# First layer's 147 contraction rows in one full pass and a quarter-array group, with slots of four chunks

## The chip, the cores and the metric

The kernel runs on one core of one Trainium2 chip. The metric is the device time of one execution in microseconds. Five engines work beside each other, each through its own queue in order: TensorE (PE, with its weight loads shown apart as PEld), VectorE (DVE), ScalarE (ACT), GpSimd (POOL) and SyncE (SP), which here only issues DMA transfers.

## The reference

Attention through 49 agents, then two dense layers over 12480 tokens of 128 values.

```python
def sm(a, b):
    s = scale * (a @ b.transpose(0, 2, 1))
    s = s - s.max(-1, keepdims=True)
    e = np.exp(s)
    return e / (e.sum(-1, keepdims=True) + 1e-09)
a2k = sm(agents, k)
agent_v = a2k @ v
q2a = sm(q, agents)
x = q2a @ agent_v                                   # 12480 x 128
h = x @ moe_w_in                                    # 128 -> 2048
g = np.where(h > 0, h, np.exp(np.minimum(h, 0)) - 1)
x = g @ moe_w_out                                   # 2048 -> 128
h = x @ moe2_w_in                                   # 128 -> 2048
g = np.maximum(h, 0) + moe2_alpha * np.minimum(h, 0)
out = g @ moe2_w_out                                # 2048 -> 128
```

## The kernel before

**Precision.** Matrix products run in fp32r, a float32 form with fewer mantissa bits, and get back what is lost by splitting: a value is written as a high part (its fp32r rounding) and a low part (the rest). A product of two split operands is three matmuls, high x high, high x low, low x high (`mm3`).

**First layer, folded.** The kernel multiplies `agent_v` with the first layer's weights once (the end of `prologue`), so that the first layer for a token is a product of its 49 softmax weights with a 49 x 2048 matrix. `pst[b]` holds the softmax weights of a block, transposed: 64 partitions with the high parts (49 agents, padded to 64), 64 with the low parts. `s1` holds the folded weights' high parts, the 49 rows once for each half, and `s1l` the low parts in the same layout. `g1` multiplies both with `pst`: two matmuls of 128 contraction rows for each chunk of 128 hidden values, 16 chunks (`NF`) a block.

**Blocks, units, slots.** The tokens come in 25 blocks (`BLOCKS`: ten of 480, fifteen of 512). Two chunks make a unit; a block has eight units (`NP`), the kernel 200 (`U`). `slot(s)` issues the work of one step: `g1` of unit s and its activations; `g1_elu` of unit s-1, which gives `g`, its fp32r rounding `gh` (on DVE for even units, on ACT for odd ones) and the rest `gl` (POOL); `g2` of unit s-`D1` (second matrix of the first layer, 6 matmuls, accumulated over the block in one PSUM bank `y`); `g3` of unit t = s-`L2` (first matrix of the second layer, 6 matmuls, and `xh` on ACT, `xl` on DVE); `g4` of unit t-`D2` (last matrix, 6 matmuls, accumulated in bank `o`, with three more for the linear part at the block's end, a copy and the store). `e` is made by two ACT steps, Relu and Exp.

**PSUM.** Eight banks: `y`, `o`, and a ring of three pairs (`hpair`), which `g1`, `g3` and `q_scores` take in turn. A pair comes free when the last engine that reads it is done.

**Softmax of later blocks.** `queries(t)` spreads the softmax of a coming block over the slots, by the table `Q_STEPS`, in units of one chunk: scores (two matmuls, L157 and L158, step 3), maximum, exponential, sum, normalisation, transposition, and at last `q_hi` (ACT) and `q_lo` (POOL), which write `pst`.

**Order.** In the prologue and the first `AUTO` slots a planner orders every engine's queue but SP's, which is as written; after these, all queues are in the order of the code. In the first slots `micro` also issues parts of `decode`, which turns the 64-bit words of the remaining weight slices into float32 high and low parts, on DVE, ACT, POOL and PE. `PE_LO` names the slices whose low part PE makes.

Of the kernel before, what the change touches and what calls it, by code (L numbers as in the profile page):

```python
# [15 lines left out]
P = 128  # L16
# [6 lines left out]
BLOCKS = [480] * 10 + [512] * 15  # L23
PIECES = [(i * 1280, 10, 128) for i in range(9)] + [(11520, 8, 120)]
NP = NF // 2
D1 = 2
D2 = 1
L2 = 11
Q_AHEAD = 24
NY = 2  # L30
WORK = 2
KRING = 4
# [7 lines left out]
    w9 w10 w11 w12 w13 w14 w15  # L40
"""
ORDER = """
    S0 T9 S1 Q2 T9 S2 Q2 T9 S3 Q2 S4 Q2 S5 Q2 D0 T9 S6 Q2 X0 E0 E1 T9 S7 Q2 T9 S8 Q2 E2 E3 T9 S9 T9 E4 A0 D1
# [15 lines left out]
def agent_attention_moe_kernel(  # L59
# [11 lines left out]
    alpha: bass.AP,  # L71
    outT: bass.AP,
):

# [16 lines left out]
    def bank(tag, bufs):  # L91
        if tag in ("m", "z"):
            return rings["mz"].tile([P, 512], F32, tag=tag, bufs=bufs, name=tag)
        return ps.tile([P, 512], F32, tag=tag, bufs=bufs, name=tag)

    def hpair():
        return rings["h"].tile([P, 2, 512], F32, tag="h", name="h")
# [5 lines left out]
        t0 += n  # L103
    NB = len(blocks)

    q_t, q_st, pst, y_ps, y_t, o_ps = {}, {}, {}, {}, {}, {}
    h_t, g_t, e_t, x_t, k_t = {}, {}, {}, {}, {}
    rings = {}

# [10 lines left out]
    s1l = const.tile([P, NF, P], F32R, name="s1l")  # L120
# [134 lines left out]
    def q_lo(b):  # L255
# [59 lines left out]
    def decode(i):  # L315
# [29 lines left out]
        parts = i in PE_LO  # L345
        u = a
        if parts:
            u = u1[j] if name == "wi1" else dec.tile([P, 4, P], F32R, tag="du", name="du")
# [70 lines left out]
    def micro(n):  # L419

        while n > 0:
            ran = False
            for x in list(flying):
                if next(x, "end") == "end":
                    flying.remove(x)
                ran = True
                n -= 1
            if len(flying) < 2 and started[0] in words:
                flying.append(decode(started[0]))
                started[0] += 1  # L430
            elif not ran:
                return
# [6 lines left out]
    w1, u1 = {}, {}  # L439

    def prologue():
        nc.sync.dma_start(out=agp, in_=agT)
        make_identity(nc, ident)
        nc.gpsimd.tensor_copy(out=plus, in_=ident)
        nc.vector.tensor_scalar(out=minus, in0=ident, scalar1=-1.0, scalar2=None, op0=ALU.mult)
        stages = [f for k in sorted(Q_STEPS) for f in Q_STEPS[k]]
        with tc.tile_pool(name="att", bufs=1) as att:
            with tc.tile_pool(name="kring", bufs=KRING) as kr, tc.tile_pool(name="vring", bufs=1) as vr, \
                    tc.tile_pool(name="sps", bufs=2, space=bass.MemoryType.PSUM) as sps, \
                    tc.tile_pool(name="mz", bufs=1, space=bass.MemoryType.PSUM) as mz:  # L450
# [9 lines left out]
                mx = att.tile([P, 2, A], F32, name="mx")  # L460
                for j in range(4):
                    w1[j] = att.tile([P, 4, P], F32, name=f"w1_{j}")
                    u1[j] = att.tile([P, 4, P], F32R, name=f"u1_{j}") if j in PE_LO else None
                pump()

                for t in range(2):
# [70 lines left out]
                for x in ORDER.split():  # L537
# [17 lines left out]
                    out=avs[:, 1, :], in0=av[1][:A, 0:P + 1], scalar=cs[:, 1:2], in1=avs[:, 0, :],  # L555
                    op0=ALU.mult, op1=ALU.add,
                )
                at = bank("o", 1)
                nc.tensor.transpose(at[:, 0:A], avs[:, 1, 0:P], ident[:A, :A])
                avn = att.tile([P, 2, AP], F32, name="avn")  # L560
                nc.gpsimd.memset(avn, 0.0)
                nc.vector.tensor_copy(out=avn[:, 0, :A], in_=at[:, 0:A])
                nc.scalar.copy(out=avn[:, 1, :A], in_=at[:, 0:A])
                avr = att.tile([P, 2, AP], F32R, name="avr")
                nc.vector.tensor_copy(out=avr, in_=avn)
                rs = att.tile([P, 1], F32, name="rs")
                nc.gpsimd.memset(rs, 0.0)
                nc.vector.tensor_scalar(out=rs[:A], in0=avs[:, 1, P:P + 1], scalar1=1e-9, scalar2=None, op0=ALU.add)
                nc.vector.reciprocal(out=rs[:A], in_=rs[:A])
                nc.vector.tensor_copy(out=rs[AP:], in_=rs[:AP])  # L570
            rings["h"] = ctx.enter_context(tc.tile_pool(name="hps", bufs=3, space=bass.MemoryType.PSUM))
            for j in range(4):
                if j % 2 == 0:
                    hp = hpair()
                wp = hp[:, j % 2, :]
                sl = slice(4 * j, 4 * j + 4)
                last = j not in PE_LO
                nc.tensor.matmul(
                    wp, avn.rearrange("p j a -> p (j a)"), w1[j].rearrange("p f c -> p (f c)"), start=True, stop=last
                )  # L580
                if not last:
                    nc.tensor.matmul(
                        wp, avr.rearrange("p j a -> p (j a)"), u1[j].rearrange("p f c -> p (f c)"),
                        start=False, stop=True,
                    )
                w4 = wp.rearrange("p (f c) -> p f c", c=P)
# [27 lines left out]
    def g1_elu(u):  # L614
        n = of(u)[2]
        g = wide("g", F32, n)
        e, h = e_t.pop(u), h_t.pop(u)
        nc.vector.scalar_tensor_tensor(out=g, in0=e, scalar=-1.0, in1=h, op0=ALU.add, op1=ALU.max)  # L618
        gh = wide("gh", F32R, n, D1 + 1)
        if u % 2:  # L620
            nc.scalar.copy(out=gh, in_=g)  # L621
        else:
            nc.vector.scalar_tensor_tensor(out=gh, in0=e, scalar=-1.0, in1=h, op0=ALU.add, op1=ALU.max)  # L623
        gl = wide("gl", F32R, n, D1 + 1)
        nc.gpsimd.tensor_tensor(out=gl, in0=g, in1=gh.bitcast(F32), op=ALU.subtract)  # L625
        g_t[u] = gh, gl

# [19 lines left out]
    def g3(u):  # L647
        b, i, n = of(u)
        yh, yl = y_t[b]
        h = hpair()[:, :, :n]  # L650
        assert WI2[i // 4] in done
        for c in range(2):
            mm3(h[:, c, :], wi2h[:, i + c, :], wi2l[:, i + c, :], yh[:, :n], yl[:, :n], True, True)
        xh, xl = wide("xh", F32R, n, D2 + 1), wide("xl", F32R, n, D2 + 1)
# [28 lines left out]
    def queries(t):  # L683
        b = t // NF
        if t % NF == 0:
            load_q(b + 2)
        for c in range(max(1, b), min(b + 3, NB)):
            for k in range(-NF, Q_AHEAD - NF) if t == 0 and c == 1 else ():
                for f in Q_STEPS.get(k, ()):
                    f(c)  # L690
            for f in Q_STEPS.get(t - NF * c + Q_AHEAD, ()):
                f(c)

    def slot(s):
# [12 lines left out]
        micro(MICRO)  # L707
        run(g1, s)
        run(g1_act, s)
        if s < U:  # L710
            queries(2 * s + 1)
        run(g4, t - D2)
        run(g2, s - D1)

    with tc.manual_schedule(engines=PINNED):
        for s in range(AUTO):
            slot(s)
    with tc.manual_schedule():
        for s in range(AUTO, U + L2 + D2):
            slot(s)  # L720


# [39 lines left out]
```

## Time and profile before

| what | value |
|---|---|
| median of 3 runs | 1191.17 us (1190.48 to 1193.3) |
| profiled execution | 1191.09 us |
| its span, first to last instruction | 1189.3 us |
| busy in the span | PE 94%, PEld 77%, DVE 68%, ACT 68%, POOL 54% |
| mean granted PE clock | 0.977 of full speed |

The profile is of one execution. A line of it names the line of the code, the engine, the operation, the tile written and those read, and the shape. Matmuls are pipelined: the distance between two starts tells the rate, and a matmul's own duration, with its modelled end, is longer. "Idle before" is the time in which the engine had nothing to do ahead of an instruction, and the name behind the arrow is what ended it.

### The profile page before, as it was taken

Reading aid. Unit: us, or ns where it says so; the run is one execution under the profiler, and the core shown is the slowest. Engines: PE = TensorE matmul, PEld = TensorE weight load, DVE = VectorE, ACT = ScalarE, POOL = GpSimd, SP = SyncE. Lnnn points to the kernel's source line nnn. Section 1 sums busy time; section 2 is a strip of 40 time slices with the busy share of each in tenths; the row PEclk is TensorE's granted clock in tenths of the full one; section 3 lists DMA queues with packets and bytes.
Section 4 is the critical chain, followed back from the end, with each engine's and each line's share of the span. In section 5 each row is a group of like instructions: output and inputs, shape, how many; then the busy total and the mean of one; then the engine's idle time right before and its main releaser. Section 6 shows DMA issues by size and latency. Waiting matters only on the chain.

```text
span 1189.3 us, 13141 instructions
## 1 busy us (share of the span) xinstructions
PE 1116.0 (94%) x4986; PEld 916.0 (77%) x4986; DVE 809.8 (68%) x977; ACT 806.2 (68%) x923; POOL 642.2 (54%) x351
## 2 busy tenths in 40 slices
PE   7866699999999999999999999999999999999998
PEld 6744588888888888878778778778777877878886
DVE  6979756666766676676667666666676667666653
ACT  3436577767776777777676777777677677777753
POOL 2667845455555555555554555555455555555530
PEclk9877799999999999999999999999999999999999
DMA  9860000000000000000000000000000000000000
GB/s 340 235 174 9 0 1 18 17 1 18 17 1 17 18 18 1 18 18 1 18 18 17 2 18 18 1 18 18 1 18 18 1 18 18 0 10 10 9 1 18
DMA packets 24077, 34.82 MB, mean 29 GB/s; under 512 B 1679, under 2 KB 16719, under 8 KB 24015
## 3 DMA queue, kind: packets, MB, share of 16 engines
q1 hardware_dynamic: 24015, 33.99, 9.0%
q8 instruction: 39, 0.64, 0.2%
q14 instruction: 23, 0.19, 0.0%
HBM read 27.60 MB, written 6.39 MB: 29 GB/s over the span
## 4 chain that ended last, share of the span: by engine, by line
PE 64%; DVE 21%; ACT 10%; issue 4%; DMA 1%; POOL 0%; SPq 0%; DVEq 0%; POOLq 0%; ACTq 0%
DVE g L618 6%; PE o L436 6%; PE o L437 6%; PE o L435 6%; PE h L435 6%; PE h L436 6%; PE y L435 6%; PE y L437 6%; PE y L436 6%; PE h L437 5%; PE h L605 5%; PE h L606 5%; DVE gh L623 5%; ACT e L612 2%; ACT gh L621 2%
## 5 line engine op out<-in xcount | busy, mean ns | idle before, releaser
L625 POOL TENSOR_TENSOR gl<-g,gh 128x1024 fp32r<-128x1024 f32 (+1 forms) x200 | 471.2, 2356 | 412.3 <-ACT gh L621 225.6
L656 DVE SCALAR_TENSOR_TENSOR xl<-h,xh 128x1024 fp32r<-128x1024 f32 (+1 forms) x200 | 239.0, 1195 | 238.4 <-ACT xh L655 236.7
L655 ACT ACTIVATE xh<-h 128x1024 fp32r<-128x1024 f32 (+1 forms) x200 | 200.2, 1002 | 126.7 <-PE h L437 126.6
L618 DVE SCALAR_TENSOR_TENSOR g<-e,h 128x1024 f32<-128x1024 f32 (+1 forms) x200 | 237.4, 1187 | 54.4 <-issue 26.0
L612 ACT ACTIVATE e<-e 128x1024 f32<-128x1024 f32 (+1 forms) x200 | 208.0, 1040 | 6.2
L611 ACT ACTIVATE e<-h 128x1024 f32<-128x1024 f32 (+1 forms) x200 | 200.0, 1001 | 10.4 <-PE h L606 5.1
L621 ACT CAST gh<-g 128x1024 fp32r<-128x1024 f32 (+1 forms) x100 | 102.8, 1028 | 150.7 <-DVE g L618 150.7
L605 PE MATMUL h<-pst,s 128*128 128x512 f32 (+1 forms) x400 | 158.2, 396 | 11.4 <-DVE gh L623 3.9
L435 PE MATMUL y<-gh,wo1h 128*128 128x512 f32 (+1 forms) x400 | 156.8, 392 | 5.6 <-DVE gh L623 5.6
L435 PE MATMUL h<-yh,wi2h 128*128 128x512 f32 (+1 forms) x400 | 156.1, 390 | 3.0 <-DVE g L618 3.0
L606 PE MATMUL h<-pst,s1l 128*128 128x512 f32 (+1 forms) x400 | 158.4, 396 | 0.0
L436 PE MATMUL y<-gl,wo1h 128*128 128x512 f32 (+1 forms) x400 | 157.3, 393 | 0.3 <-POOL gl L625 0.3
L437 PE MATMUL y<-gh,wo1l 128*128 128x512 f32 (+1 forms) x400 | 156.4, 391 | 0.0
L436 PE MATMUL o<-xl,wo2h 128*128 128x512 f32 (+1 forms) x400 | 155.7, 389 | 0.7 <-DVE xl L656 0.7
L437 PE MATMUL o<-xh,wo2l 128*128 128x512 f32 (+1 forms) x400 | 155.7, 389 | 0.0
L437 PE MATMUL h<-yh,wi2l 128*128 128x512 f32 (+1 forms) x400 | 155.6, 389 | 0.0
L435 PE MATMUL o<-xh,wo2h 128*128 128x512 f32 (+1 forms) x400 | 155.6, 389 | 0.0
L436 PE MATMUL h<-yl,wi2h 128*128 128x512 f32 (+1 forms) x400 | 155.6, 389 | 0.0
L623 DVE SCALAR_TENSOR_TENSOR gh<-e,h 128x1024 fp32r<-128x1024 f32 (+1 forms) x100 | 118.6, 1186 | 0.0
L605 PEld LDWEIGHTS h<-pst,s 128*128 128x128 f32 x400 | 76.4, 191 | 30.4 <-DVE gh L623 4.7
L435 PEld LDWEIGHTS y<-gh,wo1h 128*128 128x128 f32 x400 | 75.9, 190 | 21.8 <-issue 6.1
L435 PEld LDWEIGHTS h<-yh,wi2h 128*128 128x128 f32 x400 | 75.4, 188 | 19.3 <-ACT yh L643 3.4
(150 smaller groups left out, 1374.2 us busy)
## 6 DMA issues: line engine op xcount, KB each, us to landing
vt<-in_vm_dram SPq DMA_DIRECT2D x9, 640.0 KB, 7.1
kt<-in_kT_dram SPq DMA_DIRECT2D x8, 640.0 KB, 6.5
wi<-in_w_in_dram SPq DMA_DIRECT2D x8, 512.0 KB, 7.1
wo<-in_w_out_dram SPq DMA_DIRECT2D x8, 512.0 KB, 7.8
q<-in_qT_dram SPq DMA_DIRECT2D x15, 256.0 KB, 2.9
out_dram<-o SPq DMA_DIRECT2D x15, 256.0 KB, 2.0
q<-in_qT_dram SPq DMA_DIRECT2D x10, 240.0 KB, 3.2
out_dram<-o SPq DMA_DIRECT2D x10, 240.0 KB, 2.0
```

Source lines behind the costliest of these rows:

```text
L435: nc.tensor.matmul(out, w_hi, x_hi, start=start, stop=False)
L436: nc.tensor.matmul(out, w_hi, x_lo, start=False, stop=False)
L437: nc.tensor.matmul(out, w_lo, x_hi, start=False, stop=stop)
L605: nc.tensor.matmul(h_t[u][:, c, :], s1[:, i + c, :], pst[b][:, :n], start=True, stop=False)
L606: nc.tensor.matmul(h_t[u][:, c, :], s1l[:, i + c, :], pst[b][:, :n], start=False, stop=True)
L611: nc.scalar.activation(out=e, in_=h_t[u], func=AF.Relu, scale=-1.0)
L612: nc.scalar.activation(out=e, in_=e, func=AF.Exp, scale=-1.0)
L618: nc.vector.scalar_tensor_tensor(out=g, in0=e, scalar=-1.0, in1=h, op0=ALU.add, op1=ALU.max)
L623: nc.vector.scalar_tensor_tensor(out=gh, in0=e, scalar=-1.0, in1=h, op0=ALU.add, op1=ALU.max)
L625: nc.gpsimd.tensor_tensor(out=gl, in0=g, in1=gh.bitcast(F32), op=ALU.subtract)
L655: nc.scalar.activation(out=xh, in_=h, func=AF.Relu)
L656: nc.vector.scalar_tensor_tensor(out=xl, in0=h, scalar=0.0, in1=xh.bitcast(F32), op0=ALU.max, op1=ALU.subtract)
```

## The change

The first layer's contraction has 3 x 49 = 147 rows: high x high, high x low and low x high. The kernel before spends 256 rows on them, in two passes. The changed kernel puts 115 of them into one pass of 128 rows, and the other 32 into a 32-row matmul:

- `pst` keeps its 64 + 64 rows. The 15 padding agents are now copies of agents 0 to 14, so that rows 49 to 63 hold their high softmax weights again, which meet the low parts of the folded weights. Two more rows (agents 15 and 16) come by a small DMA. `Q0` = 17.
- `psq[b]` holds the high softmax weights of agents 17 to 48 four times, in partitions 0, 32, 64 and 96, by four DMAs (`q_place`, a new step behind `q_lo`).
- `s1q` holds the low parts for these 32 agents, of four chunks in the four groups of 32 partitions. `g1` now serves two units: four full matmuls and four of 32 contraction rows, each with its own partitions and PSUM bank.
- The end of the prologue normalises `agent_v` first, makes the quarter weights by 16 small matmuls into the four column groups (`hq`), and `s1` and `s1q` on DVE.
- A slot is two units (four chunks) long. `g1_split` is cut off from `g1_elu`. The order in a slot, the places of the softmax steps (`ask`), `L2` (11 to 10) and the rings of `gh`, `gl`, `xh`, `xl` change; `q_scores` falls at the end of a slot, behind `g4`.

```diff
-D1 = 2
-D2 = 1
-L2 = 11
+L2 = 10
+Q0 = 17
+GBUFS = 4
+XBUFS = 3
...
-PE_LO = (0, 2, 4)
+PE_LO = (4,)
...
-AUTO = 13
+AUTO = 12
...
+    def q_place(b):
+        n = blocks[b][1]
+        psq[b] = sm.tile([P, BLK], F32R, tag="psq", bufs=2, name="psq")
+        eng = nc.sync if b else nc.scalar
+        for g in range(4):
+            eng.dma_start(out=psq[b][32 * g:32 * g + 32, :n].bitcast(F32), in_=pst[b][Q0:A, :n].bitcast(F32))
+        eng.dma_start(out=pst[b][P - 15:P - 30 + Q0, :n].bitcast(F32), in_=pst[b][15:Q0, :n].bitcast(F32))
...
-        21: [q_lo],
+        21: [q_lo, q_place],
...
+        nc.scalar.copy(out=agp[:, A:], in_=agp[:, :AP - A])
...
+            hq = hpair()[:, 0, :].rearrange("p (k c) -> p k c", c=P)
+            hp = []
             for j in range(4):
                 if j % 2 == 0:
-                    hp = hpair()
...
-                nc.scalar.activation(out=s1[:, sl, :], in_=w4, func=AF.Copy, scale=rs)
+                for g in range(4):
+                    nc.tensor.matmul(
+                        hq[32 * g:32 * g + 32, j, :], avq[:, g, :], w1[j][:, g, :], start=True, stop=True
+                    )
+            hi = [att2.tile([P, 4, P], F32R, name=f"hi{j}") for j in range(2)]
+            nc.vector.tensor_copy(out=hi[1], in_=hq)
+            nc.vector.tensor_tensor(out=s1q, in0=hq, in1=hi[1].bitcast(F32), op=ALU.subtract)
+            for j in range(4):
+                w4 = hp[j // 2][:, j % 2, :].rearrange("p (f c) -> p f c", c=P)
+                nc.vector.tensor_copy(out=hi[j % 2], in_=w4)
                 nc.vector.scalar_tensor_tensor(
-                    out=s1l[:, sl, :], in0=w4, scalar=rs, in1=s1[:, sl, :].bitcast(F32),
-                    op0=ALU.mult, op1=ALU.subtract,
+                    out=s1[:, 4 * j:4 * j + 4, :], in0=hi[j % 2].bitcast(F32), scalar=low, in1=w4,
+                    op0=ALU.mult, op1=ALU.add,
                 )
...
     def g1(u):
         b, i, n = of(u)
-        h_t[u] = hpair()[:, :, :n]
-        for c in range(2):
-            nc.tensor.matmul(h_t[u][:, c, :], s1[:, i + c, :], pst[b][:, :n], start=True, stop=False)
-            nc.tensor.matmul(h_t[u][:, c, :], s1l[:, i + c, :], pst[b][:, :n], start=False, stop=True)
+        for v in range(2):
+            h_t[u + v] = hpair()[:, :, :n]
+            for c in range(2):
+                nc.tensor.matmul(h_t[u + v][:, c, :], s1[:, i + 2 * v + c, :], pst[b][:, :n], start=True, stop=False)
+        for g in range(4):
+            p = slice(32 * g, 32 * g + 32)
+            nc.tensor.matmul(
+                h_t[u + g // 2][:, g % 2, :], s1q[p, i // 4, :], psq[b][p, :n], start=False, stop=True
+            )
...
+        def ask(k):
+            micro(MICRO)
+            if s < U:
+                queries(2 * s + k)
+
         t = s - L2
-        micro(MICRO)
-        run(g1_elu, s - 1)
+        ask(0)
+        run(g1_split, s - 1)
         run(g3, t)
-        if s < U:
-            queries(2 * s)
-        micro(MICRO)
-        run(g1, s)
+        run(g1, s) if s < U else None
         run(g1_act, s)
-        if s < U:
-            queries(2 * s + 1)
-        run(g4, t - D2)
-        run(g2, s - D1)
+        run(g1_act, s + 1)
+        run(g4, t - 1)
+        ask(1)
+        run(g1_elu, s)
+        run(g1_split, s)
+        run(g2, s - 2)
+        ask(2)
+        run(g1_elu, s + 1)
+        run(g2, s - 1)
+        run(g3, t + 1)
+        run(g4, t)
+        ask(3)
```

## Rows read from the trace of the kernel before

**Rows 1.** The page: busy time of PE, and its granted clock in 40 slices.

```profile
PE 1116.0 (94%) x4986; PEld 916.0 (77%) x4986; DVE 809.8 (68%) x977; ACT 806.2 (68%) x923; POOL 642.2 (54%) x351
PEclk9877799999999999999999999999999999999999
```

**Rows 2.** Timeline, first `g1` matmul of neighbouring blocks: start us, us, engine, line, instruction.

```profile
338.51 0.38 PE L605 MATMUL h<-pst,s 128*128 128x480 f32 x1
...
379.63 0.38 PE L605 MATMUL h<-pst,s 128*128 128x480 f32 x1
...
718.96 0.40 PE L605 MATMUL h<-pst,s 128*128 128x512 f32 x1
...
762.44 0.40 PE L605 MATMUL h<-pst,s 128*128 128x512 f32 x1
```

**Rows 3.** Waits of PE from 150 us on: us in total, times, longest.

```profile
PE h L157 <- DVE gh L623: 25.0, 22, 1.5
```

**Rows 4.** Timeline of PE around two blocks' first score matmul (480 and 512 tokens).

```profile
322.67 0.38 PE L605 MATMUL h<-pst,s 128*128 128x480 f32 x1
322.89 0.37 PE L606 MATMUL h<-pst,s1l 128*128 128x480 f32 x1
324.35 0.46 PE L157 MATMUL h<-qh,ag 128*128 128x480 f32 x1 [1.08 <-DVE gh L623]
...
745.79 0.39 PE L605 MATMUL h<-pst,s 128*128 128x512 f32 x1
746.02 0.40 PE L606 MATMUL h<-pst,s1l 128*128 128x512 f32 x1
747.49 0.47 PE L157 MATMUL h<-qh,ag 128*128 128x512 f32 x1 [1.07 <-DVE gh L623]
```

**Rows 5.** Stretches: length, busy PE, PEld, DVE, ACT, POOL (xcount), PEclk, DMA, GB/s.

```profile
100.00:110.00 10.00, 3.71 (x11) 2.82 (x12) 9.88 (x12) 7.05 (x9) 7.61 (x6) 0.58 0.00 0
...
150.00:160.00 10.00, 9.66 (x45) 7.98 (x43) 5.50 (x5) 6.47 (x8) 2.76 (x2) 1.00 0.01 2
```

**Rows 6.** Groups by line: xcount | busy us, mean ns of one | idle before, releasers.

```profile
L656 DVE SCALAR_TENSOR_TENSOR xl<-h,xh 128x1024 fp32r<-128x1024 f32 (+1 forms) x200 | 239.0, 1195 | 238.4 <-ACT xh L655 236.7
L618 DVE SCALAR_TENSOR_TENSOR g<-e,h 128x1024 f32<-128x1024 f32 (+1 forms) x200 | 237.4, 1187 | 54.4 <-issue 26.0 <-ACT e L612 24.8 <-POOL pst L258 2.0
L623 DVE SCALAR_TENSOR_TENSOR gh<-e,h 128x1024 fp32r<-128x1024 f32 (+1 forms) x100 | 118.6, 1186 | 0.0
...
L612 ACT ACTIVATE e<-e 128x1024 f32<-128x1024 f32 (+1 forms) x200 | 208.0, 1040 | 6.2
L655 ACT ACTIVATE xh<-h 128x1024 fp32r<-128x1024 f32 (+1 forms) x200 | 200.2, 1002 | 126.7 <-PE h L437 126.6
L611 ACT ACTIVATE e<-h 128x1024 f32<-128x1024 f32 (+1 forms) x200 | 200.0, 1001 | 10.4 <-PE h L606 5.1 <-DVE s1l L588 2.5 <-DVE gh L623 2.2
```

**Rows 7.** Timeline of the prologue, loads of TensorE where the array's shape changes.

```profile
48.02 0.19 PEld L410 LDWEIGHTS o<-du,plus 128*128 128x128 f32 x1 [0.19 <-issue]
...
48.44 0.39 PEld L524 LDWEIGHTS y<-vt,S 128*49 128x49 f32 x4 [0.24 <-issue]
...
53.37 0.29 PEld L506 LDWEIGHTS o<-ident,mb 49*128 49x128 f32 x2 [0.19 <-DVE cs L547]
```

**Rows 8.** Timeline of PE in the prologue's score stage: seven matmuls, each with a load.

```profile
25.79 0.94 PE L481 MATMUL sp<-agd,kt 128*128 128x98 f32 x7
```

**Rows 9.** The low softmax part by line, one store's issue, and the stores' landing.

```profile
L258 POOL TENSOR_TENSOR pst<-st,pst 64x512 fp32r<-64x512 f32 (+1 forms) x25 | 31.9, 1275 | 2.0
...
607.92 0.34 SPq L676 DMA_DIRECT2D out_dram<-o  x1
...
out_dram<-o SPq DMA_DIRECT2D x15, 256.0 KB, 2.0
```

**Rows 10.** The folded weights' low part by line, and the first `g1` matmul's time.

```profile
L588 DVE SCALAR_TENSOR_TENSOR s1l<-h,rs,s 128x512 fp32r<-128x512 f32 x4 | 3.0, 744 | 0.0
...
L605 PE MATMUL h<-pst,s x400: 378/392/769, 90.6 to 1145.0; 128*128 128x512 f32 x80, 128*128 128x480 f32 x54
```

More of the change, by code (lines that the diff above doesn't have):

```diff
@@ L119, in agent_attention_moe_kernel @@
     s1 = const.tile([P, NF, P], F32R, name="s1")
-    s1l = const.tile([P, NF, P], F32R, name="s1l")
+    s1q = const.tile([P, 4, P], F32R, name="s1q")
+    low = const.tile([P, 1], F32, name="low")
     lin = const.tile([P, P], F32, name="lin")
@@ L347, in decode @@
         if parts:
-            u = u1[j] if name == "wi1" else dec.tile([P, 4, P], F32R, tag="du", name="du")
+            u = dec.tile([P, 4, P], F32R, tag="du", name="du")
         if i in U_POOL:
@@ L445, in prologue @@
         nc.vector.tensor_scalar(out=minus, in0=ident, scalar1=-1.0, scalar2=None, op0=ALU.mult)
+        nc.vector.tensor_reduce(
+            out=low, in_=minus.bitcast(F32).rearrange("p (h c) -> p h c", h=2)[:, :, A:], axis=AX.XY, op=ALU.add
+        )
         stages = [f for k in sorted(Q_STEPS) for f in Q_STEPS[k]]
         with tc.tile_pool(name="att", bufs=1) as att:
+            att2 = att
             with tc.tile_pool(name="kring", bufs=KRING) as kr, tc.tile_pool(name="vring", bufs=1) as vr, \
@@ L462, in prologue @@
                     w1[j] = att.tile([P, 4, P], F32, name=f"w1_{j}")
-                    u1[j] = att.tile([P, 4, P], F32R, name=f"u1_{j}") if j in PE_LO else None
                 pump()
@@ L557, in prologue @@
                 )
+                rs = att.tile([A, 1], F32, name="rs")
+                nc.vector.tensor_scalar(out=rs, in0=avs[:, 1, P:P + 1], scalar1=1e-9, scalar2=None, op0=ALU.add)
+                nc.vector.reciprocal(out=rs, in_=rs)
+                nc.vector.tensor_scalar(
+                    out=avs[:, 0, 0:P], in0=avs[:, 1, 0:P], scalar1=rs, scalar2=None, op0=ALU.mult
+                )
                 at = bank("o", 1)
-                nc.tensor.transpose(at[:, 0:A], avs[:, 1, 0:P], ident[:A, :A])
+                nc.tensor.transpose(at[:, 0:A], avs[:, 0, 0:P], ident[:A, :A])
@@ L560, in prologue @@
                 avn = att.tile([P, 2, AP], F32, name="avn")
[L561 to L568, printed above, removed]
@@ L569, in prologue @@
-                nc.vector.reciprocal(out=rs[:A], in_=rs[:A])
-                nc.vector.tensor_copy(out=rs[AP:], in_=rs[:AP])
+                avq = att.tile([P, 4, 32], F32, name="avq")
+                nc.vector.memset(avn[:, 1, A:], 0.0)
+                nc.vector.tensor_copy(out=avn[:, :, :A], in_=at[:, 0:A].unsqueeze(1).to_broadcast([P, 2, A]))
+                nc.scalar.copy(out=avq, in_=at[:, Q0:A].unsqueeze(1).to_broadcast([P, 4, 32]))
+                nc.vector.tensor_copy(out=avn[:, 0, A:], in_=at[:, 0:15])
@@ L571, in prologue @@
+                nc.scalar.copy(out=avn[:, 1, A:A + Q0 - 15], in_=at[:, 15:Q0])
             rings["h"] = ctx.enter_context(tc.tile_pool(name="hps", bufs=3, space=bass.MemoryType.PSUM))
+            hq = hpair()[:, 0, :].rearrange("p (k c) -> p k c", c=P)
+            hp = []
             for j in range(4):
                 if j % 2 == 0:
-                    hp = hpair()
-                wp = hp[:, j % 2, :]
-                sl = slice(4 * j, 4 * j + 4)
-                last = j not in PE_LO
+                    hp.append(hpair())
+                wp = hp[-1][:, j % 2, :]
@@ L578, in prologue @@
                 nc.tensor.matmul(
-                    wp, avn.rearrange("p j a -> p (j a)"), w1[j].rearrange("p f c -> p (f c)"), start=True, stop=last
+                    wp, avn.rearrange("p j a -> p (j a)"), w1[j].rearrange("p f c -> p (f c)"), start=True, stop=True
                 )
-                if not last:
+                for g in range(4):
                     nc.tensor.matmul(
-                        wp, avr.rearrange("p j a -> p (j a)"), u1[j].rearrange("p f c -> p (f c)"),
-                        start=False, stop=True,
-                    )
@@ L616, in g1_elu, with g1_split @@
         g = wide("g", F32, n)
+        gh = wide("gh", F32R, n, GBUFS)
         e, h = e_t.pop(u), h_t.pop(u)
         nc.vector.scalar_tensor_tensor(out=g, in0=e, scalar=-1.0, in1=h, op0=ALU.add, op1=ALU.max)
-        gh = wide("gh", F32R, n, D1 + 1)
+        if u % 2 == 0:
+            nc.vector.scalar_tensor_tensor(out=gh, in0=e, scalar=-1.0, in1=h, op0=ALU.add, op1=ALU.max)
+        g_t[u] = g, gh
+    def g1_split(u):
+        n = of(u)[2]
+        g, gh = g_t[u]
         if u % 2:
             nc.scalar.copy(out=gh, in_=g)
-        else:
-            nc.vector.scalar_tensor_tensor(out=gh, in0=e, scalar=-1.0, in1=h, op0=ALU.add, op1=ALU.max)
-        gl = wide("gl", F32R, n, D1 + 1)
+        gl = wide("gl", F32R, n, GBUFS)
         nc.gpsimd.tensor_tensor(out=gl, in0=g, in1=gh.bitcast(F32), op=ALU.subtract)
@@ L653, in g3 @@
             mm3(h[:, c, :], wi2h[:, i + c, :], wi2l[:, i + c, :], yh[:, :n], yl[:, :n], True, True)
-        xh, xl = wide("xh", F32R, n, D2 + 1), wide("xl", F32R, n, D2 + 1)
+        xh, xl = wide("xh", F32R, n, XBUFS), wide("xl", F32R, n, XBUFS)
         nc.scalar.activation(out=xh, in_=h, func=AF.Relu)
@@ L699, in run @@
                 f(u)
+        def ask(k):
+            micro(MICRO)
+            if s < U:
+                queries(2 * s + k)
         t = s - L2
-        micro(MICRO)
-        run(g1_elu, s - 1)
+        ask(0)
+        run(g1_split, s - 1)
         run(g3, t)
-        if s < U:
-            queries(2 * s)
-        micro(MICRO)
-        run(g1, s)
+        run(g1, s) if s < U else None
         run(g1_act, s)
-        if s < U:
-            queries(2 * s + 1)
-        run(g4, t - D2)
-        run(g2, s - D1)
+        run(g1_act, s + 1)
[10 more added lines that the diff above has]
+        ask(3)
     with tc.manual_schedule(engines=PINNED):
-        for s in range(AUTO):
+        for s in range(0, AUTO, 2):
             slot(s)
     with tc.manual_schedule():
-        for s in range(AUTO, U + L2 + D2):
+        for s in range(AUTO, U + L2 + 2, 2):
             slot(s)
```

8 lines of the change are left out of this document (4 added, 4 removed).

## The prediction

> **What bounds the kernel now.** I read the page first: TensorE (PE) is busy 94% of the span and its granted clock is at the full level (2.4 GHz) in nearly every slice [rows 1]. A busy PE need not be at its peak, so I looked next at the distance between starts. In a block of 512 tokens one matmul starts 0.23 us after the other (745.79, 746.02), in a block of 480 tokens 0.22 (322.67, 322.89) [rows 4]. By the code a block has 181 matmuls: 32 in the first layer (two for each of 16 chunks), 48 in `g2`, 48 in `g3`, 51 in `g4`, 2 for the scores. 181 x 0.23 = 41.6 us; a block really takes 762.44 - 718.96 = 43.48 us, and one of 480 tokens takes 379.63 - 338.51 = 41.12 us against 181 x 0.22 = 39.8 [rows 2]. So the steady part runs at the rate of PE's stream, with 1.3 to 1.9 us missing in each block. The waits say where: PE's first score matmul (L157) waits for VectorE (DVE) `gh` 22 times, 25 us in all [rows 3]. The page counts less than is lost, because a matmul's modelled end covers part of the gap; start to start the gap is 747.49 - 746.02 = 1.47 us, and 324.35 - 322.89 = 1.46 us with 480 tokens, 1.24 us over the usual distance in both [rows 4]. 22 x 1.24 = 27 us.
>
> Before about 150 us another limit holds: from 100 to 110 us DVE is busy 9.88 of 10 us, and PE 3.71; from 150 on PE is busy 9.66 of 10 at full clock [rows 5]. There the weights are still being decoded, and a matmul saved is worth nothing. So I count savings from block 2 on, and half for block 1.
>
> **The change part by part.** *Scores at the slot's end.* `q_scores` takes a pair of PSUM banks from the ring of three. Today it asks right after `g1`, for the pair that `g1_elu` of the unit before still reads; that is the stall. In the new order it takes the pair of unit s, after `g4`, `g2`, `g2`, `g3`, `g4`. From the end of `g1` these are 30 matmuls x 0.23 = 6.9 us on PE. The pair is free after Relu 1.00, Exp 1.04 (ScalarE, ACT), `g` 1.19 and `gh` 1.19 on DVE = 4.4 us [rows 6]. So it is free 2.5 us early, and the 1.24 us go. What is late next? The next slot's `g3` takes the pair of unit s+1: its `g` comes behind `gh` of s, 4.4 + 1.2 = 5.6 us, and a softmax step between them still fits into the 1.3 us that are left. The next `g1` needs the pair that `xl` of t+1 frees: `xh` 1.00 + `xl` 1.20 after `g3` [rows 6], with some 0.3 us of hand-overs (my estimate) 2.5 us, against `g4`, `g3` and two matmuls = 14 x 0.23 = 3.2 us. This is the thinnest cover, 0.7 us. If it is gone, each slot of four chunks waits by what is missing.
>
> *First layer packed.* For four chunks, eight matmuls become four full ones and four of 32 rows, each in its own quarter of the array. I call the time that the four quarters add G. Four full matmuls go, 4 x 0.23 = 0.92 us (0.88 with 480 tokens). No row shows two matmuls in the array at once, so G has to be bounded. From below: they stream together and nothing is lost, 0.23 us. From above: one after another. In between lies what rows show of a change of the array's shape. L410 is a full 512-column matmul between two of 49 columns: its weight load starts at 48.02, after the loader sat idle 0.19 us for nothing the profile shows, and the next load starts at 48.44, after 0.24 us [rows 7]. Load to load that is 0.42 us where the stream takes 0.23: 0.19 more for one change of shape. A 49-row matmul in between (L506) shows the same 0.19 us ahead of its load [rows 7]. Ordinary loads lie hidden beside the matmul before; across a change they don't. Every group has two changes, in and out, so G = 0.21 (512 columns at 2.4 GHz) + 2 x 0.20 = 0.61 us, and 0.60 with 480. The nearest row for a load by itself is the score stage of the prologue: seven matmuls with a 128-column load each and few columns to stream take 0.94 us, about 0.11 us from one to the next [rows 8]. If the four quarter loads go one after another, G = 0.61 + 3 x 0.11 = 0.94 us. If the four streams do too, G = 0.61 + 3 x 0.23 = 1.30 us. I take 0.61: the quarters read different partitions and write different banks, and the shape changes are shown by rows.
>
> The Trainium skill, TensorEngine Tiling, section Key Properties, speaks both ways: a change of tiling mode drains the array, and tiles load weights and multiply independently. The first half agrees with the trace, 0.19 us at L410; the second no run here shows. The Trainium skill, TensorE: Matmul & The Clock Gate, Part 3: Packing small matmuls, gives 3.07 times for four row tiles of 512 columns; by that figure alone the four quarters would take an estimated 4 x 0.23 / 3.07 = 0.30 us, and the sum below would come out near 1110 us.
>
> *Placing DMAs.* `q_place` adds five transfers a block on SyncE's (SP's) queue (ACT's for block 0), behind `q_lo`. `q_lo` takes 1.28 us on POOL; an output store's issue on SP 0.34 us; a store of 256 KB lands in 2.0 us [rows 9], and these are 64 KB and less. 1.28 + 5 x 0.34 + 2.0 = 5.0 us. From the asking place to the next slot's `g1` PE has `g2`, `g2`, `g3`, `g4`, `g3` = 30 x 0.23 = 6.9 us. So they cost nothing; with the cover gone, a late landing would stop PE once in each block. Behind SP's wait stand the query load for two blocks ahead and the output store of the next slot but one, neither urgent.
>
> *Engines and slots.* Wide work on DVE, ACT and POOL stays as it is, per slot of four chunks: DVE 2 x 1.19 + 1.19 + 2 x 1.20 = 6.0 us, ACT seven steps of 1.0 us [rows 6], some softmax steps more. The slot falls from 43.48 / 4 = 10.9 us to about 10.2 us, so PE stays the bound. Deeper rings (`GBUFS`, `XBUFS`) add no instruction. The gaps of a group are shorter than today's 1.24 us stalls, through which the granted clock stays at its upper level of 2.4 GHz [rows 1], so I count no loss there.
>
> *Startup and lag.* `s1`, `s1q` and their high parts are now ten DVE steps where four `s1l` stood, 0.744 us each [rows 10]: 6 x 0.7 = 4 us more on an engine that is full there [rows 5]; ACT loses four. Sixteen small matmuls and up to eight changes of shape come ahead of the first `g1` on PE, bounded by 16 x 0.23 + 8 x 0.2 = 5.3 us. `L2` is one unit shorter: 12 matmuls, 2.8 us, come earlier into a stretch where PE has room. Bounds -3 to +10 us; I take +4, the DVE steps.
>
> **The sum.** A block of 480 tokens loses 1.24 + 4 x (0.88 - 0.60) = 2.36 us, eight of them (2 to 9) 18.9. A block of 512 loses 1.24 + 4 x (0.92 - 0.61) = 2.48 us, thirteen of them (10 to 22) 32.2. The last two have no scores ahead: 2 x 1.24 = 2.5. Block 1 gives half, 1.2. Together 54.8 us, less 4 us of startup: 50.8. The profiled execution took 1191.09 us, as good as the median of 1191.17 us: 1191.1 - 50.8 = 1140.3 us, rounded to 1140.
>
> **The rivals.** All change G in 94 groups (23.5 blocks x 4), except the last.
> - *Loads one after another* (G 0.94): 94 x 0.33 = 31 us back, 1171 us. For it: a load's 0.11 us is paid at every change of shape. Against it: the quarters are different rows.
> - *No price for the changes of shape* (G 0.23): 94 x 0.38 = 36 us more, 1104 us. Against it: rows 7.
> - *The quarters stream one after another* (G 1.30): 94 x 0.69 = 65 us back, 1205 us, slower than before. The packing then costs more than it saves, and the scores' 27 us don't cover it. It decides from G = 0.61 + 50.8/94 = 1.15 us on. No row speaks against it, as none shows two at once.
> - *The stall only moves*: the scores or the next `g1` wait for a pair somewhere else, so that 27 us stay: 1140 + 27 = 1167 us. For it: three pairs, and `g1` now holds two at once. Against it: covers of 2.5 and 0.7 us.
>
> **How the numbers follow.** Forecast 0.50, loads in series 0.22, no price for changes 0.09, stall moved 0.09, streams in series 0.10. The range goes from 1103 (just under no price) to 1175 (loads in series or stall moved, with the startup at its worse end); streams in series are left out, and what lies under 1103 or between 1175 and 1205. A measurement of this kernel tells about 0.3% from no change, 3.6 us. The first four cases are all faster by more; of the last I give 0.03 to no change (its loss is 1%, but G may lie near 1.15) and 0.07 to slower. Faster 0.90, same 0.03, slower 0.07.
>
> **What would show it.** Steps right: no wait at the score matmuls; blocks of about 41.0 us (512) and 38.8 us (480) from one block's first `g1` matmul to the next's; four quarter matmuls that start within a few hundredths of a microsecond, and about 0.2 us idle of the loader ahead of the first quarter load and of the next full load. Quarter loads 0.11 us apart mean loads in series; quarter matmuls 0.23 us apart mean streams in series. A wait of `g1` for `xl`, or of the full matmul for a DMA, means that a cover was too thin. A first `g1` matmul later than 100 us (now at 90.6 [rows 10]) would put the startup at its worse end.

## The result and the profile after

The changed kernel takes 1141.54 us (median of 4 runs, 1138.96 to 1142.04) against 1190.83 us of the kernel before in the same comparison. The ratio is 0.9581, with a 95% interval from 0.9558 to 0.9604. The forecast was 1140 us.

The page's first lines of the changed kernel, as [rows 1] of before:

```profile
span 1139.7 us, 13430 instructions
PE 1089.4 (96%) x5016; PEld 854.2 (75%) x5016; DVE 870.5 (76%) x985; ACT 806.7 (71%) x921; POOL 640.7 (56%) x351
PEclk9777789999999999999999999999999999999999
```

PE is the bound still, and busier. The timeline of PE gives the first `g1` matmul of neighbouring blocks (L629 is what L605 was in [rows 2]): the first of all, that of block 2, then two blocks of 480 and two of 512 tokens.

```profile
104.66 0.49 PE L629 MATMUL h<-pst,s 128*128 128x480 f32 x1 [0.46 <-DVE s L610]
...
182.17 0.38 PE L629 MATMUL h<-pst,s 128*128 128x480 f32 x1
...
336.89 0.38 PE L629 MATMUL h<-pst,s 128*128 128x480 f32 x1
375.58 0.38 PE L629 MATMUL h<-pst,s 128*128 128x480 f32 x1
...
694.35 0.39 PE L629 MATMUL h<-pst,s 128*128 128x512 f32 x1
735.22 0.39 PE L629 MATMUL h<-pst,s 128*128 128x512 f32 x1
```

A block takes 38.69 and 40.87 us where it took 41.12 and 43.48. The other end of the sum is the startup. In the kernel before, block 2 starts at:

```profile
174.25 0.38 PE L605 MATMUL h<-pst,s 128*128 128x480 f32 x1
```

From there to the end it needed 1189.3 - 174.25 = 1015.1 us, now 1139.7 - 182.17 = 957.5 us: 57.5 us gained. Ahead of it, 7.9 us are lost.

The scores, in the timeline of PE (as in [rows 4]), follow the matmuls ahead of them at the usual distance, and the waits of PE from 160 us to the end (us in total, times, longest) have one row, where before the 22 waits for `gh` stood [rows 3]:

```profile
723.20 0.40 PE L450 MATMUL o<-xh,wo2l 128*128 128x512 f32 x1
723.44 0.39 PE L162 MATMUL h<-qh,ag 128*128 128x512 f32 x1
723.67 0.40 PE L163 MATMUL h<-ql,ag 128*128 128x512 f32 x1
```

```profile
PE o L449 <- DVE xl L689: 0.7, 1, 0.7
```

And this is a group of four quarters (L632), between four full matmuls (L629) and the next `g4`, in the timeline of all engines:

```profile
704.27 1.10 PE L629 MATMUL h<-pst,s 128*128 128x512 f32 x4
...
705.30 0.19 PEld L632 LDWEIGHTS h<-psq,s1q 32*128 32x128 f32 x4 [0.37 <-issue]
705.30 0.50 PE L632 MATMUL h<-psq,s1q 32*128 32x512 f32 x4
705.73 0.19 PEld L448 LDWEIGHTS o<-xh,wo2h 128*128 128x128 f32 x1 [0.24 <-ACT xh L688]
705.73 0.50 PE L448 MATMUL o<-xh,wo2h 128*128 128x512 f32 x1
...
706.07 0.39 PE L449 MATMUL o<-xl,wo2h 128*128 128x512 f32 x1
```

The four loads are over within 0.19 us, as long as one, and the four matmuls within 0.50 us: loads and streams run together. The loader sits idle 0.37 us ahead of the group and 0.24 us behind it. From the last full matmul (704.27 + 1.10 - 0.40 = 704.97) to L449 are 1.10 us; less two full matmuls of 0.23 that leaves G = 0.64 us. The three distances in it are 0.33, 0.43 and 0.34 us: against 0.23, 0.10 us are lost ahead of the group, 0.20 behind it and 0.11 one matmul later.

### The profile page after: what moved, and what is told of

The parts are those of the page before. It is cut to its first block, busy times and chain, and to the rows that moved or that the text cites. A ratio compares the mean times of both kernels' runs of the same rounds, so it can differ in the third digit from the quotient of the medians.

```text
span 1139.7 us, 13430 instructions
## 1 busy us (share of the span) xinstructions
PE 1089.4 (96%) x5016; PEld 854.2 (75%) x5016; DVE 870.5 (76%) x985; ACT 806.7 (71%) x921; POOL 640.7 (56%) x351
## 4 chain that ended last, share of the span: by engine, by line
PE 88%; DVE 8%; issue 1%; POOL 1%; ACT 1%; DMA 1%; SPq 0%; DVEq 0%; POOLq 0%; ACTq 0%
PE o L448 10%; PE o L450 8%; PE o L449 8%; PE h L448 8%; PE h L449 8%; PE h L450 8%; PE h L629 8%; PE y L448 8%; PE y L449 8%; PE y L450 8%; PE h L632 4%; PE z L541 1%; DVE S L529 1%; DVE pm L508 1%; DMA wi<-in_w_in_dram 1%
## 5 line engine op out<-in xcount | busy, mean ns | idle before, releaser
L639 ACT ACTIVATE e<-h 128x1024 f32<-128x1024 f32 (+1 forms) x200 | 199.1, 996 | 35.3 <-PE h L632 32.2
L448 PE MATMUL o<-xh,wo2h 128*128 128x512 f32 (+1 forms) x400 | 165.4, 413 | 0.0
L449 PE MATMUL y<-gl,wo1h 128*128 128x512 f32 (+1 forms) x400 | 157.1, 393 | 2.6 <-POOL gl L658 2.5
L449 PE MATMUL o<-xl,wo2h 128*128 128x512 f32 (+1 forms) x400 | 155.6, 389 | 0.7 <-DVE xl L689 0.7
L449 PE MATMUL h<-yl,wi2h 128*128 128x512 f32 (+1 forms) x400 | 156.3, 391 | 0.0
L629 PE MATMUL h<-pst,s 128*128 128x512 f32 (+1 forms) x400 | 111.1, 398 | 6.4 <-DVE s L610 2.2
L448 PEld LDWEIGHTS o<-xh,wo2h 128*128 128x128 f32 x400 | 75.1, 188 | 34.7 <-ACT xh L688 17.1
L629 PEld LDWEIGHTS h<-pst,s 128*128 128x128 f32 x400 | 75.8, 192 | 24.2 <-issue 3.2
L449 PEld LDWEIGHTS y<-gl,wo1h 128*128 128x128 f32 x400 | 75.7, 189 | 20.1 <-POOL gl L658 3.6
```

What stands on the lines that cost most here:

```text
L448: nc.tensor.matmul(out, w_hi, x_hi, start=start, stop=False)
L629: nc.tensor.matmul(h_t[u + v][:, c, :], s1[:, i + 2 * v + c, :], pst[b][:, :n], start=True, stop=False)
L639: nc.scalar.activation(out=e, in_=h_t[u], func=AF.Relu, scale=-1.0)
```

## The experiments

Blocks are read from the first `g1` matmul of one 512-token block to that of the next.

**The scores back behind `g1`.**

```diff
-                f(c)
+                if f is not q_scores:
+                    f(c)
...
         run(g1_act, s + 1)
+        if s < U:
+            ask_scores(2 * s + 3)
         run(g4, t - 1)
```

The first lines, in `queries`, leave the scores out there; `ask_scores` asks for them alone.

> The changed kernel with the scores of a coming block asked right behind g1 and its activations, as in the kernel before, instead of at the slot's end; nothing else is moved. Theory (the stall depends on which pair of banks the scores take): they now take the pair of g3 of the same slot, which xh (1.00 us) and xl (1.20 us) free some 2.5 us after that g3 ends, while PE has only the four full matmuls and the group, about 1.6 us. So PE stalls about 1 us at the first score matmul of some 22 blocks: 1141.5 + 22 = about 1163 us. Rival (the longer slot or the deeper rings cured the stall, the place of the scores is nothing): 1141 us, no wait at the scores.

Measured: 1206.25 us, ratio to before 1.0126 (1.0058 to 1.0195). PE waits for `xl` at the scores 21 times, as the theory has it, but the loss is three times as large. The waits of PE from 200 us on, the timeline around one of them, and two stretches (columns as in [rows 5]):

```profile
PE h L162 <- DVE xl L689: 40.5, 21, 2.2
```

```profile
615.78 2.03 DVE L242 COPY r<-r 32x16 f32<-32x16 f32 x1
616.66 0.51 PE L632 MATMUL h<-psq,s1q 32*128 32x512 f32 x4
617.85 1.22 DVE L689 SCALAR_TENSOR_TENSOR xl<-h,xh 128x1024 fp32r<-128x1024 f32 x1
619.12 0.50 PE L162 MATMUL h<-qh,ag 128*128 128x512 f32 x1 [1.96 <-DVE xl L689]
```

```profile
620.00:624.00 4.00, 4.00 (x12) 3.16 (x11) 3.47 (x4) 1.28 (x2) 2.08 (x1) 0.57 0.00 0
624.00:632.00 8.00, 8.00 (x37) 6.03 (x36) 2.64 (x3) 4.92 (x6) 2.13 (x2) 1.00 0.13 32
```

A small copy on DVE, which takes 2.03 us here, stands ahead of `xl`, so the gap is 619.12 - 616.66 = 2.46 us and not about 1.5. Behind it the granted clock is at 1.2 GHz for most of 4 us: the matmuls start 0.43 us apart there. A block takes 44.44 us, 3.6 more than in the changed kernel. The clock falls like this behind 14 of the 21 stalls: behind all twelve from 575 us on, and behind two of the nine before. So the place of the scores is worth more than I gave it: a stall is longer than I worked out, and most of them cost the clock too.

**The scores alone, in the kernel before.**

```diff
         run(g4, t - D2)
         run(g2, s - D1)
+        if s < U:
+            ask_scores(2 * s + 1)
```

`queries` leaves the scores out, as in the run above.

> The kernel before with one thing changed: the scores (and no other softmax step) go to the end of its slot, behind g4 and g2. Theory: the 1.24 us at 22 blocks go and nothing takes their place, 1191 - 27 = 1164 us, and no wait of PE for gh at the scores. Rival (the wait moves to the next g1 or g3): 1185 to 1191 us, with the wait under another line.

Measured: 1157.56 us, ratio 0.9717 (0.9664 to 0.9771). Nothing takes the place of the wait; from 150 to 1150 us PE waits for no one. The first `g1` matmuls of block 2 and of two 512-token blocks:

```profile
172.97 0.38 PE L605 MATMUL h<-pst,s 128*128 128x480 f32 x1
...
697.07 0.39 PE L605 MATMUL h<-pst,s 128*128 128x512 f32 x1
...
739.13 0.39 PE L605 MATMUL h<-pst,s 128*128 128x512 f32 x1
```

A block takes 42.06 us, 1.4 less. This one move, alone, gives 33 us where the whole change gives 49.

**Four full matmuls in place of the four quarters.**

```diff
-            nc.tensor.matmul(
-                h_t[u + g // 2][:, g % 2, :], s1q[p, i // 4, :], psq[b][p, :n], start=False, stop=True
-            )
+            nc.tensor.matmul(h_t[u + g // 2][:, g % 2, :], s1[:, i + g, :], pst[b][:, :n], start=False, stop=True)
```

> The changed kernel with the four quarter matmuls replaced by four full ones of 128 rows (s1 and pst a second time, so the first layer's low parts are left out and its high part counts twice); order, rings and placing DMAs stay. Theory: G is 0.63 us (0.60 with 480 tokens) in the changed kernel and 4 x 0.23 = 0.92 us (0.88) here, 0.28 to 0.29 us more in some 95 groups: 1141.5 + 27 = about 1168 us. Rival (the whole gain came from the scores and the order, the packing gives nothing): 1141 us.

Measured: 1164.16 us, ratio 0.9773 (0.9709 to 0.9837), so the quarters are worth 22.6 us.

```profile
180.76 0.38 PE L629 MATMUL h<-pst,s 128*128 128x480 f32 x1
...
706.36 0.39 PE L629 MATMUL h<-pst,s 128*128 128x512 f32 x1
...
748.52 0.39 PE L629 MATMUL h<-pst,s 128*128 128x512 f32 x1
```

A block takes 42.16 us: (42.16 - 40.87) / 4 = 0.32 us a group. Against the scores alone the blocks are nearly the same (42.06), but block 2 starts 7.8 us later. So the rest of the change, without the quarters, costs some 7 us (1164.16 against 1157.56), and 33 and 22.6 add up to more than 49.

**One full matmul in place of the four quarters.**

```diff
-        for g in range(4):
-            p = slice(32 * g, 32 * g + 32)
-            nc.tensor.matmul(...)
+        nc.tensor.matmul(h_t[u + 1][:, 1, :], s1[:, i + 3, :], pst[b][:, :n], start=False, stop=True)
...
```

> The changed kernel with the four quarter matmuls replaced by one full matmul (the low parts are left out, and one chunk in four gets its high part twice). It streams as long as the four quarters together, without a change of the array's shape. Theory (two changes of shape cost 0.40 us a group): 95 x 0.40 = 38 us less, about 1103 us. Rival (another engine or a pair of banks holds the slot up as soon as PE gets faster): at least 1120 us, with waits of PE for xl, gh or gl in each slot.

Measured: 1097.27 us, ratio 0.9211 (0.9162 to 0.9261). Without the two changes of shape a block takes:

```profile
176.42 0.38 PE L629 MATMUL h<-pst,s 128*128 128x480 f32 x1
...
705.84 0.40 PE L629 MATMUL h<-pst,s 128*128 128x512 f32 x1
...
745.12 0.40 PE L629 MATMUL h<-pst,s 128*128 128x512 f32 x1
```

39.28 us, (40.87 - 39.28) / 4 = 0.40 us less a group. From 200 to 1090 us PE waits once, 0.7 us, for `xl`: even here no other engine binds.

**All four quarters in the same rows of the array.**

```diff
-            p = slice(32 * g, 32 * g + 32)
+            p = slice(0, 32)
```

> The changed kernel with all four quarter matmuls of a group in the same quarter of the array (partitions 0 to 31 of the quarter weights and of the placed softmax weights for each, so the low parts of three chunks in four are wrong); their number, size and place in the order stay. Theory (the four stream together because they lie in four quarters): now they stream one after another, G = 0.63 + 3 x 0.23 = 1.32 us, 95 x 0.69 = 65 us more: about 1207 us. Rival (a 32-row matmul is cheap by itself, wherever it lies): 1141 us.

Measured: 1203.24 us, ratio 1.0106 (1.0085 to 1.0126), slower than before. The group in the timeline:

```profile
707.22 0.76 PEld L632 LDWEIGHTS h<-psq,s1q 32*128 32x128 f32 x4 [0.37 <-issue]
707.22 1.19 PE L632 MATMUL h<-psq,s1q 32*128 32x512 f32 x4
```

1.19 us instead of 0.50, four loads in 0.76 us instead of 0.19. That is the rival of streams in series, made on purpose; the forecast gave it 1205 us. What pays in the changed kernel is that the four lie in four quarters of the array.

**Two groups of two quarters.**

```diff
         for v in range(2):
             ...
+            for g in (2 * v, 2 * v + 1):
+                p = slice(32 * g, 32 * g + 32)
+                nc.tensor.matmul(h_t[u + v][:, g % 2, :], s1q[p, i // 4, :], psq[b][p, :n], start=False, stop=True)
-        for g in range(4):
-            ...
```

> The changed kernel with the group of four quarters cut in two groups of two, each behind its own two full matmuls; what is computed stays. Theory (each entry into and exit from the 32-row shape costs about 0.20 us, whatever the group's size, and a group streams 0.21 us): a slot has four changes of shape instead of two and one stream more, 95 x 0.63 = 60 us more, about 1201 us. Rival (a change of shape costs nothing, what is lost in the changed kernel's group is something else): one stream more, 95 x 0.21 = 20 us, about 1161 us.

Measured: 1197.59 us, ratio 1.0058 (1.0038 to 1.0078). A block takes 43.31 us:

```profile
728.00 0.39 PE L629 MATMUL h<-pst,s 128*128 128x512 f32 x1
...
771.31 0.39 PE L629 MATMUL h<-pst,s 128*128 128x512 f32 x1
```

(43.31 - 40.87) / 4 = 0.61 us more a slot. The second group costs as much as the first: two more changes of shape and one more stream. Behind both groups the loader sits idle 0.24 us here for nothing that the profile shows, so in the changed kernel the same idle time needs no wait for `xh` to explain it.

**High parts on ACT** (five `nc.vector.tensor_copy(out=hi..)` become `nc.scalar.copy`).

> The changed kernel with the five high-part copies at the prologue's end on ACT instead of DVE; everything else stays. Theory (the startup, 8 us longer to the start of block 2, is DVE's six added steps): DVE loses 5 x 0.68 = 3.4 us where it is busy 8 to 9.9 of 10 us, block 2 starts some 3 us earlier, about 1138 us. Rival (the longer startup comes from PE, whose clock stands at its lower level while the weighted sum of the values runs, and from waits at the first g3): 1141 us, block 2 at 182 us as now.

Measured: 1140.45 us (1135.56 to 1141.47), ratio 0.9565 (0.9542 to 0.9587). Block 2 starts at 182.34 us, as before the edit, so the theory isn't borne out. The run is no clean test of it: block 1 starts 4.3 us later (141.77 against 137.48), behind a wait of PE of 4.8 us for a softmax step, and its own time is shorter by as much.

**Placing DMAs for block 0 alone** (`q_place` returns for later blocks).

> The changed kernel with the five placing DMAs of a block done for block 0 alone; all later blocks multiply with block 0's copy (their low parts are wrong, and the two extra rows are not filled). Theory (the placing lies beside other work): no difference that can be measured, 1138 to 1145 us. Rival (a late landing holds PE once a block): up to 24 x 0.5 us less, 1130 us.

Measured: 1138.06 us (1136.38 to 1141.9), ratio 0.9563 (0.9544 to 0.9582), with the same blocks. The placing costs nothing in the time that can be told apart.

**The small softmax copies as maxima** (`tensor_copy(out, x)` becomes `tensor_tensor(out, x, x, op=max)` in `q_max`, `q_norm_2`, `q_norm_4`).

> The changed kernel with the three small softmax copies of DVE (maximum, sum, reciprocal, 32 partitions x 15 or 16) written as a maximum of the operand with itself: the same values, another DVE operation. In the changed kernel's profile such copies take 0.2 us or, beside a POOL subtraction, over 2 us, 89 us in all. Theory (in the steady part PE sets the time and DVE has room, so that only the startup can gain; there the copy of 2.2 us at 146 us holds up the wait of PE for the first g3): DVE some 70 us less busy, steady blocks as before (40.87 us), 2 to 5 us less: about 1138 us. Rival (DVE's chain binds somewhere in the steady part): blocks below 40.5 us and 1130 us or less.

Measured: 1142.4 us, ratio 0.9595 (0.9577 to 0.9612). The edit didn't do what it was for: a copy takes as long in the other form (by line: xcount | busy, mean ns of one | idle before).

```profile
L242 DVE TENSOR_TENSOR r<-r 32x16 f32<-32x16 f32 (+1 forms) x25 | 45.5, 1821 | 0.8
```

So it says nothing of what a faster DVE would bring.

**Early scores with those maxima**, the first experiment once more with this edit.

> The kernel of the early scores with the three small DVE copies written as maxima, as in the other run. In the early-scores run the stall at the scores is 2.46 us start to start, because a DVE copy of 2.0 us stands ahead of xl, and the granted clock falls to 1.2 GHz behind each of them. Theory (the stall shrinks to about 1.6 us, near the 1.47 us of the kernel before, through which the clock stayed up): 22 x 1.05 us above the changed kernel, about 1164 us, clock full through the steady part. Rival (the clock falls with the scores at that place, whatever the copy): 1195 us or more.

Measured: 1202.17 us, ratio 1.0099 (1.0076 to 1.0122). As the copy is no shorter, the gap is 617.35 - 614.90 = 2.45 us again, and the clock falls again; whether a shorter gap there would leave it up stays open.

```profile
614.90 0.51 PE L632 MATMUL h<-psq,s1q 32*128 32x512 f32 x4
...
617.35 0.59 PE L162 MATMUL h<-qh,ag 128*128 128x512 f32 x1 [1.94 <-DVE xl L689]
```

**More slots ordered by the planner** (`AUTO` 16 instead of 12).

> The changed kernel with AUTO 16 in place of 12, so that the planner and not the code orders two more slots; nothing else. Theory (the startup loses 3.7 us of PE at the first g3, at the change from the planner's order to the code's, and the lower clock after it): the planner fills the wait, block 2 starts some 4 us earlier: about 1137 us. Rival (the startup is bound by decode work on DVE and POOL): 1141 us.

Measured: 1143.27 us, ratio 0.9606 (0.959 to 0.9622). Block 2 starts at 184.63 us, later rather than earlier. The wait of PE ahead of the first `g3`, which the edit was to fill, is still there, 3.7 us long.

**Without the quarter weights** (`s1q` set to zero; the 16 small matmuls and two DVE steps left out).

> The changed kernel with the quarter weights set to zero instead of made at the prologue's end: the 16 small matmuls into the column groups and two DVE steps are left out (so the low parts of 32 agents are), the steady part is untouched. Theory (the first g1, at 104.7 us instead of 90.6, waits for this chain, and the blocks behind it start late by it): the first g1 at about 97 us and block 2 some 3 us earlier than 182 us, about 1138 us. Rival (the startup is held by the decoding of the weights on DVE and POOL, or by PE's lower clock, and not by the first g1): the first g1 may come earlier, block 2 stays at 181 to 184 us, 1141 us.

Measured: 1140.72 us, ratio 0.9587 (0.957 to 0.9604). The first `g1` comes 8.7 us earlier, and block 2 only 1.5:

```profile
95.96 0.46 PE L623 MATMUL h<-pst,s 128*128 128x480 f32 x1 [1.42 <-DVE s L604]
...
180.63 0.38 PE L623 MATMUL h<-pst,s 128*128 128x480 f32 x1
```

No version that still computes the same can be told to be faster than the changed kernel.

## Why the prediction was right, step by step

**What bounds the kernel.** Right. Both terms of the gain lie in PE's stream, and the time went down by what PE was spared. With one full matmul for the quarters it goes on down to 1097 us with no new wait.

**Scores at the slot's end.** Right in mechanism, too small in size. The forecast took the gap alone, 1.24 us a block. The scores-alone run gains 43.48 - 42.06 = 1.42 us a block. Two things were missing. The two gaps that were read, 1.46 and 1.47 us, are short ones; in 14 of the 22 blocks of the kernel before it is 1.53 us or more, as here:

```profile
789.39 0.40 PE L606 MATMUL h<-pst,s1l 128*128 128x512 f32 x1
790.92 0.47 PE L157 MATMUL h<-qh,ag 128*128 128x512 f32 x1 [1.13 <-DVE gh L623]
```

And the matmul behind the stall is late too: L158 follows L157 after 0.31 us in the kernel before, and 0.23 us now. The covers held: no wait of `g3` or `g1` for a pair of banks in the steady part. The early-scores run shows what a missing cover costs: there the stall comes back as a wait for `xl`, larger than I worked out, because a softmax step on DVE stood ahead of `xl`. In the cover of 0.7 us I had left such a step out; it held all the same, with no wait of `g1` for `xl`.

**The group's price.** Right, and near the row that it was taken from. G was put at 0.61 us and measures 0.64; 0.40 us for two changes of shape came from L410 [rows 7], and the run without them measures 0.40. It holds for the sum and not for each side: I gave 0.20 us to the way in and as much to the way out, and the starts of the matmuls show 0.10 and 0.31. That one row doubled came out so close is in part luck. The loader's idle time ahead of the group is 0.37 us, where I had looked for 0.2. The loads, which I had to bound between one and four times 0.11 us, take as long as one. The Trainium skill, TensorEngine Tiling, section Key Properties, says that tiles load weights and multiply independently; that agrees with the trace, 0.19 us for four loads and 0.50 for four matmuls. In the same section the Trainium skill says that a change of tiling mode drains the array; these runs show no drain as such, but the price of a change and its way back, 0.40 us a group. The estimate from the 3.07 times of the Trainium skill, TensorE: Matmul & The Clock Gate, Part 3: Packing small matmuls, 0.30 us for the four, was 0.34 us too low, most of what the two changes cost; the measurement decides.

**The rivals.** Loads in series and no price for the changes are ruled out by the group's rows and the one-full run. Streams in series is what the same-quarter run makes, 1203.24 us where 1205 was worked out. The stall that only moves is ruled out by the scores-alone run, and by PE's one wait in the changed kernel.

**Placing, rings.** Right in the steady part, where PE waits for no DMA. The sign of a cover too thin shows once, ahead of block 1:

```profile
137.48 0.46 PE L629 MATMUL h<-pst,s 128*128 128x480 f32 x1 [1.56 <-DMA pst<-pst]
```

With the placing for block 0 alone block 2 starts no earlier (182.88 us), so it isn't to be seen in the time.

**Startup.** The step that failed. I took +4 us for DVE's six added steps, less 1.2 that block 1 gives: 2.8 us to the start of block 2. It is 7.9 us (182.17 - 174.25). The sign that I had named for the worse end came, a first `g1` later than 100 us (104.66). The cause that I gave isn't shown: with the five copies on ACT block 2 starts as before. Nor is it the first `g1`, which is 14 us later: made 8.7 us earlier it moves block 2 by 1.5. Of the 7.9 us, 6.5 are lost by the start of block 1 (137.48 against 131.02), and 1.5 in block 1.

In block 1 one stop of PE tells the versions of the changed kernel apart, ahead of the first `g3`, which needs `yh` from ACT. In the changed kernel, and then in the four-full run:

```profile
149.53 0.99 ACT L656 CAST gh<-g 128x960 fp32r<-128x960 f32 x1 [5.12 <-DVE g L647]
150.43 0.55 ACT L676 CAST yh<-y 128x480 fp32r<-128x480 f32 x1
151.04 0.77 PE L448 MATMUL h<-yh,wi2h 128*128 128x480 f32 x1 [3.67 <-ACT yh L676]
```

```profile
148.04 0.56 ACT L673 CAST yh<-y 128x480 fp32r<-128x480 f32 x1 [0.62 <-PE y L450]
148.65 0.48 PE L448 MATMUL h<-yh,wi2h 128*128 128x480 f32 x1 [0.65 <-ACT yh L673]
```

In ACT's queue `yh` stands behind a `gh` that waits 5.1 us for DVE; in the four-full run it doesn't. Behind the long stop the granted clock is at its lower level for part of the stretch from 150 to 160 us, again in the changed kernel first:

```profile
150.00:160.00 10.00, 8.80 (x30) 6.38 (x31) 3.71 (x4) 5.46 (x7) 2.88 (x2) 0.71 0.01 2
```

```profile
150.00:160.00 10.00, 8.87 (x39) 7.24 (x40) 8.12 (x10) 7.19 (x8) 5.91 (x4) 1.00 0.00 0
```

With this stop block 1 takes 44.69 us in the changed kernel, and 41.53 in the four-full run, which so starts block 2 earlier, at 180.76 us, though in the steady part its matmuls cost more. The run with one full matmul (176.42) has a short stop too, 0.6 us. The kernel before has a long one, 3.0 us, so it isn't what sets the changed kernel back. Two runs keep the long stop and make the group dearer, and block 2 moves back: 185.16 us with the quarters in series, 186.65 with two groups. So PE's work does count in the startup, where I had given it nothing. But with the short stop, too, four full matmuls, the same work as before, start block 2 7.8 us later than the scores alone do (172.97). What remains between these two are the slots of four chunks, the order and the prologue's other edits (`PE_LO`, the normalisation). Which of them it is, these runs don't settle.

**The sum.** The steady part and the tail gain 57.5 us where 53.6 stood in the sum (18.9 + 32.2 + 2.5), and the startup loses 5.1 us more than given. Over half of the 3.9 us lies in the tail. The last block's first `g1`, in the kernel before, with four full matmuls, and in the changed kernel:

```profile
1108.07 0.39 PE L605 MATMUL h<-pst,s 128*128 128x512 f32 x1
```

```profile
1085.32 0.39 PE L629 MATMUL h<-pst,s 128*128 128x512 f32 x1
```

```profile
1061.92 0.39 PE L629 MATMUL h<-pst,s 128*128 128x512 f32 x1
```

From there to the end are 81.2, 78.9 and 77.7 us. So 2.3 us come without the quarters, with the new order and the shorter `L2`, whose 2.8 us I had counted as nothing. The two errors, 3.9 and 5.1 us, nearly cancel; that the time came out closer than its terms is luck.

## What to carry to other kernels

Ask of a scratch ring who reads the buffer that an occasional user gets, and move that user to where the reader is long done: one move gave two thirds of this gain. Quarter-array matmuls pay here when the four lie in different quarters, but entering and leaving the shape costs about 0.40 us a group, nearly two full matmuls of 512 columns, so gather four in one group rather than two in each of two. The price of a change can stand in a corner of the trace that has nothing to do with it: the 49-column matmuls of the prologue gave the price of the group within 0.03 us. A gain in the steady part is not the gain of the whole: the startup of a kernel wants its own look at who waits for whom.

## What the runs showed of the hardware that I had not expected

With the scores asked early, stalls of 2.43 to 2.50 us on PE, start to start and once a block, are each followed by the clock at 1.2 GHz from 575 us on (0.57 of full speed over 4 us). Stalls as long don't always do it: before 575 us seven of nine, of 2.31 to 2.67 us, leave the clock up. The kernel before goes through one of 1.46 to 1.89 us in nearly every block at full clock.

Some small DVE steps on 32 partitions x 16 values take 0.2 us, or last until the POOL subtraction beside them ends; the mean of L242 is 1.8 us. In the last early-scores run:

```profile
613.64 2.37 POOL L658 TENSOR_TENSOR gl<-g,gh 128x1024 fp32r<-128x1024 f32 x1
614.01 2.03 DVE L242 TENSOR_TENSOR r<-r 32x16 f32<-32x16 f32 x1
```

Both end at about 616.0. A copy and a maximum of an operand with itself behave alike, and so does L232, the sum of two such operands, at 22 of its 24 places in the changed kernel. The reciprocal (L241, 0.24 us) beside the same subtraction keeps its length. Why some wait for POOL and others don't was not tried.
